# Attention outputs transposed by DMA, a wide warm-up, earlier final waits and one add on POOL in a TensorE-bound attention and feed-forward kernel

## The chip, the cores and the metric

The kernel runs on one core of a Trainium2 chip. The metric is the device time of one execution in microseconds (us). The time of a run is about 1.7 us longer than the span of its trace (580.16 against 578.4 us for the profiled run of the kernel before).

## The reference

For x of 2048 tokens by 576 features, in bfloat16:

```python
xn = _layernorm(x)
s  = A(xn)            # 32 heads of 18, causal window of 256 keys, softmax, then @ wo
g  = silu(B(xn))      # h = sigmoid(xn @ w_gate) * (xn @ w_up); h @ w_down   (F = 4608)
out = x + s * g
```

## The kernel before

The kernel describes its work as a graph of operations, each with an estimated length, and a list scheduler in the kernel itself places them on the engines' in-order queues before anything runs. So a change of one operation can move the order on every engine. Tokens are handled in four chunks of 512, each of four blocks of 128. The core's feed-forward matmuls fill the time in which attention waits. The contraction of 128 rows is split into two halves of 64 rows which TensorE (PE) runs side by side; "a pair" is one matmul on each half.

The parts that the change touches:

```python
# start: warm-up matmuls on zeros, pairs of 256 columns   [NWARM = 60]
zero = self.hT[:, 0, 0:2 * P]
z = op("DVE", 600, lambda e: e.memset(zero, 0.0), "init:zero", prio=0)
for i in range(NWARM):
    ...pair(eng, self.halves(h, 2 * P), lambda r, t: zero[r, 0:P], lambda r, t: zero[r, :], True, True)
    w = op("PE", 220 if i < 18 else 110, f_warm, f"warm:{i}", ...)   # left out once the first real matmul is placed

# end of attention: TensorE transposes each of the four blocks, DVE evicts, then the output projection   [NOT = 2]
tr = op("PE", KB * 29.5, f_tr, f"otr:{qb}", ...)
te = op("DVE", dve_ns(KB * P, 1.9), f_te, f"ote:{qb}", deps=[tr, do], prio=1)
wo = self.row_proj("wo", qb, h2, lambda r, k, so=so: self.oT[r, so, k, :], ..., [te, ...])

# end of a token block: x + s * g, then the store
q3 = op("DVE", dve_ns(w, 2.0), lambda e: e.tensor_tensor(xf, xf, t, ALU.add), f"fq3:{nm}", deps=[q2, o_dx], prio=2)

# end of SyncE's program: wait for every DMA semaphore ("lane")
if e == "SP":
    for i, n in enumerate(lane_cnt):
        if n > 0:
            eng.wait_ge(lanes[i], n)
    eng.nop()
```

The last token block is finished in two column parts of 384 and 192 (`c0 == 0` is the first). One more part matters, though the change does not touch it: the q and k heads are moved into place by 160 small SBUF-to-SBUF DMAs, `qk<-qd`, which **POOL** issues.

```python
o = self.dma(dst, src, ..., f"dma:sp:{c}:{u}:{w}:{gi}", ("qk", par, gi), deps=[ev, war, self.op_qz], prio=1, eng="POOL")
```

The softmax here doesn't subtract the row's maximum and nothing guards it: scores larger than these inputs give would overflow.

Of the kernel before, what the change touches and what calls it, by code (L numbers as in the profile page):

```python
# [5 lines left out]
ALU = mybir.AluOpType  # L6

S = 2048
D = 576
# [21 lines left out]
NVS = 12  # L31
VH = DH + 1
VSZ = (H // 2) * VH
NOT = 2
NQS = 4
NKX = 2
NEX = 8
# [15 lines left out]
NQD = 2  # L53
NFIN = 2
NTAIL = 96
NWARM = 60
PARTS = ((0, 1), (1, 2), (2, 4))
NQK = 5

DMA_ISSUE_NS = {"SP": 640.0, "POOL": 520.0, "ACT": 650.0}  # L60
# [164 lines left out]
class Builder:  # L225
# [153 lines left out]
    def load_x(self, c, i=0):  # L379
        if c == 0:  # L380
            for i in range(BPC):
                self.x_dma[i] = (self.dma(self.x0[:, i, :], self.x[i * P:(i + 1) * P, :], P * D * 2, f"dma:x{i}", ("x0", i), prio=0),
                                 self.x0[:, i, :])
            return
        st = c * BPC + i
        slots, dd = [], []
        for _ in range(2):
            s_, d_ = self.r_xr.produce()
            slots.append(s_)
            dd += d_  # L390
        assert slots[1] == slots[0] + 1
        o = self.dma(self.xr[:, slots[0]:slots[0] + 2, :],
                     self.x[st * P:(st + 2) * P, :].rearrange("(t p) d -> p t d", p=P),
                     2 * P * D * 2, f"dma:x{st}", ("x", slots[0]), deps=[dd, self.hm[6] if c == 1 else None], prio=5)
        o.slack = 5000.0
        for j in range(2):
            self.x_dma[st + j] = (o, self.xr[:, slots[j], :])
# [9 lines left out]
    def build_consts(self):  # L407
        op = self.op
        self.op_negh = op("DVE", 60, lambda e: e.memset(self.neghalf[:, :], -0.5), "init:neghalf", prio=0)
        o1 = op("POOL", 200, lambda e: e.memset(self.ident[:, :], 0.0), "init:ident1", prio=0)  # L410
        o2 = op("POOL", 200, lambda e: e.affine_select(
            self.ident[:, :], self.ident[:, :], pattern=[[1, SW]], compare_op=ALU.not_equal, fill=1.0, base=0,
            channel_multiplier=-1), "init:ident2", deps=[o1], prio=0)
        self.op_ident = op("POOL", 200, lambda e: e.affine_select(
            self.ident[:, :], self.ident[:, :], pattern=[[1, SW]], compare_op=ALU.not_equal, fill=1.0, base=SW,
            channel_multiplier=-1), "init:ident3", deps=[o2], prio=0)
        zero = self.hT[:, 0, 0:2 * P]
        z = op("DVE", 600, lambda e: e.memset(zero, 0.0), "init:zero", prio=0)  # L418
        self.op_tab = op("ACT", 1500, lambda e: e.activation(self.tring[:, 0, 0:1], zero[:, 0:1], ACTF.Exp), "init:tab",
                         deps=[z], prio=0)  # L420
        h = self.pool_f.hold()
        w = None
        for i in range(NWARM):
            def f_warm(eng):
                return pair(eng, self.halves(h, 2 * P), lambda r, t: zero[r, 0:P], lambda r, t: zero[r, :], True, True)
            w = op("PE", 220 if i < 18 else 110, f_warm, f"warm:{i}", deps=[z], prio=4, acq=None if i else h, odeps=[w])
            w.filler = h
            h.release(w)

        wq, wk, wv = (self.wqkv[:, i * D:(i + 1) * D] for i in range(3))  # L430
        self.op_wqk = [self.load_nat(self.wqk[:, :, i, :], w, "dma:wqk", ("wqk", i), 5) for i, w in enumerate((wq, wk))]
        self.op_wqk += self.load_rem(self.wqkr[:, :], (wq, wk), "dma:wqkr", ("wqkr",), 5)
        for o in self.op_wqk:
            o.slack = 2500.0
        self.op_wv = [self.load_nat(self.wv_sb[:, :, :], wv, "dma:wv", ("wv",), 6)]
        self.op_wv += self.load_rem(self.wvr[:, :], (wv[:, 0:288], wv[:, 288:D]), "dma:wvr", ("wvr",), 6)
        for o in self.op_wv:
            o.slack = 5000.0
        self.op_wqk4 = [op("DVE", 420, lambda e: e.tensor_copy(self.wq4[:, 1:KB, :, :], self.wqk[:, :, :, 512:D]), "init:wq4",
                           deps=self.op_wqk, prio=2)]  # L440
        for t in range(2):
            for i in range(2):
                self.op_wqk4.append(op("DVE", 130, lambda e, t=t, i=i: e.tensor_copy(
                    self.wq4[ROWS[t], 0, i, :], self.wqkr[ROWS[i], 512:D]), f"init:wq4:{t}{i}", deps=self.op_wqk, prio=2))
# [24 lines left out]
    def build_ln(self, c):  # L469
# [3 lines left out]
        for i in range(BPC):  # L473
            st = c * BPC + i
            if c and i % 2 == 0:
# [17 lines left out]
            ap = op("DVE", 430, lambda e, ss=ss, x_in=x_in, sn=sn: e.tensor_scalar(  # L493
                self.xnr[:, sn, RD:XW], x_in, self.mv[:, ss, 0:1], self.rstd[:, ss, :],
                ALU.subtract, ALU.mult), f"ln:ap:{st}", deps=[rs, ag, dn], prio=pr)
            if c:
                dup = op("DVE", 180, lambda e, sn=sn: e.tensor_copy(self.xnr[:, sn, 0:RD], self.xnr[:, sn, RD:2 * RD]),
                         f"ln:dup:{st}", deps=[ap], prio=pr)
            else:
                dup = op("POOL", 260, lambda e, ss=ss, x_in=x_in, sn=sn: e.tensor_scalar(  # L500
                    self.xnr[:, sn, 0:RD], x_in[:, 0:RD], self.mv[:, ss, 0:1], self.rstd[:, ss, :],
                    ALU.subtract, ALU.mult), f"ln:dup:{st}", deps=[rs, ag, dn], prio=pr)
            if c:
                self.r_xr.release(i % 2, ap)
            self.r_st.release(ss, ap)
            self.r_st.release(ss, dup)
            if c:
                fl = self.flip(self.xnT[:, xs, :, i * P:(i + 1) * P], self.xnr[:, sn, :], f"flip:x:{st}", ("fx", xs, i),
                               deps=[dup, war], prio=2)
# [278 lines left out]
    def build_wo(self, c):  # L788
# [3 lines left out]
                 deps=[self.op_on[(c, 0)], self.otr_last], prio=1)  # L792
        for i in range(BPC):
            qb = c * BPC + i
            h = self.pool_s.hold()
            so, do = self.r_oT.produce()

            def f_tr(eng, i=i, h=h):
                return self.transposes(eng, h, lambda r, o: self.o_tok[r, i, o:o + P])
            tr = op("PE", KB * 29.5, f_tr, f"otr:{qb}", deps=[[self.op_on[(c, hg)] for hg in range(NHG)], dup, self.op_ident, do],  # L800
                    prio=1, acq=h)
            last.append(tr)

            def f_te(eng, h=h, so=so):
                dst = self.oT[:, so, :, :].rearrange("p k (t c) -> p t k c", t=2)
                return eng.tensor_copy(dst, self.tr_src(h))
            te = op("DVE", dve_ns(KB * P, 1.9), f_te, f"ote:{qb}", deps=[tr, do], prio=1)
            h.release(te)

            h2 = self.pool_s.hold()  # L810
            ss = i
            war = [self.op_q2[qb - BPC]] if c else []

            wo = self.row_proj("wo", qb, h2, lambda r, k, so=so: self.oT[r, so, k, :], self.wo_sb, self.wor,
                               [te, self.op_wo_w, war])
            self.r_oT.release(so, wo)

            def f_se(eng, ss=ss, h2=h2):
                dst = self.s_attn[:, ss, :].rearrange("p (t c) -> p t c", t=2)
                return eng.activation(dst, self.both(h2, 288), ACTF.Copy, scale=0.25)  # L820
            se = op("ACT", act_ns(D), f_se, f"sev:{qb}", deps=[wo], prio=1)
            h2.release(se)
            self.op_s[qb] = se
        self.otr_last = last

    def build_ffn(self, c):
# [40 lines left out]

        def gate_up(ft, h, half, acq, part=None, deps=()):
            sw, fc = slots[ft // WG], slice((ft % WG) * P, (ft % WG + 1) * P)
            b0, b1 = (0, BPC) if part is None else PARTS[part]  # L870
            t0, n = b0 * P, (b1 - b0) * P
            xin = self.op_xnT[c][b0:b1]

# [24 lines left out]
        if early:  # L898
            weights(0)
            weights(1)  # L900
            hs = [self.pool_f.hold() for _ in range(2)] + [self.pool_s.hold()]
            his = [None] * early
            for part in range(len(PARTS)):
                los = [gate_up(ft, hs[ft], 0, None if part else hs[ft], part, [his[ft]]) for ft in range(early)]
                for ft in range(early):
                    u = his[ft] = gate_up(ft, hs[ft], 1, None, part, [los[ft]])
                    if part == len(PARTS) - 1:
                        tail(ft, hs[ft], u)
                    if part == len(PARTS) - 1 and ft == 1:
                        self.r_w.release(slots[0], u)  # L910
        for ft in range(early, NFT):
            if ft % WG == 0 and ft // WG not in slots:
                weights(ft // WG)
# [50 lines left out]
    def build_final(self, sb, h, f2, c0=0, n=288):  # L964
# [36 lines left out]
            h.release(w0)  # L1001
            h.release(th1)
        self.op_q2[sb] = q2
        q3 = op("DVE", dve_ns(w, 2.0), lambda e: e.tensor_tensor(xf, xf, t, ALU.add), f"fq3:{nm}", deps=[q2, o_dx], prio=2)  # L1004
        self.r_th.release(st, q3)
        if c0 == 0:
            self.fq3 = []
# [99 lines left out]
    def emit(self):  # L1107
# [10 lines left out]
        for e in ENGS:  # L1118
            for o in self.prog[e]:
# [5 lines left out]
                else:  # L1125
                    cnt[e] += 1
                    o.tok = (("E", e), cnt[e])

        def semof(key):
            return lanes[key[1]] if key[0] == "L" else self.sem[key[1]]  # L1130

        def run_engine(e, eng):
            known = {}
            for o in self.prog[e]:
                waits = {}
                for d in o.deps:
                    k, v = d.tok
# [8 lines left out]
                if o.needs_tok:  # L1146
                    ins.then_inc(semof(o.tok[0]), 16 if o.lane is not None else 1)
            if e == "SP":
                for i, n in enumerate(lane_cnt):
                    if n > 0:  # L1150
                        eng.wait_ge(lanes[i], n)
                eng.nop()

        with nc.Block() as block:
# [61 lines left out]
```

## Time and profile before

| | before |
|---|---|
| time, median of 4 runs (3 at the time of the prediction: 579.93) | 580.25 us |
| span of the trace | 578.4 us |
| PE busy | 569.9 us |
| first, last matmul start | 1.15, 573.51 us |
| last matmul start to end of program | 4.9 us |

From the page of the kernel before: the span; busy time with share of the span and number of instructions; the granted clock in tenths over 40 slices; and the shares of the chain that ended last.

```profile
span 578.4 us, 21485 instructions
...
PE 569.9 (99%) x9542; PEld 362.2 (63%) x9542; DVE 345.5 (60%) x837; ACT 267.8 (46%) x379; POOL 179.9 (31%) x290
...
PEclk9999999999999999999999999999999999999999
...
PE 97%; DVE 2%; issue 1%; ACT 0%; POOL 0%; DVEq 0%
```

PE is busy nearly throughout and is nearly the whole chain. The ends of matmuls in a profile are modelled, so the busy share alone doesn't show lost time, and I also read PE's start-to-start steps in the trace: 108 ns for a matmul of 64x512 and 61 ns for 64x288, two at a time, with only about 9.5 us lost over the whole run.

The attention-output transposes, from the view of the tile o_tok (durations in ns as minimum, median, maximum; then first and last start in us):

```profile
L550 PE MATMUL ps<-ident,o_tok x160: 186/190/199, 114.0 to 451.7; 64*128 64x64 bf16 x160
```

The profile gives each a length of 190 ns, but they start 14.5 ns apart, so 160 of them take 2.3 us of PE.

The start, from PE's timeline (start us, length us, engine, line, operation, count, and in brackets the idle time before):

```profile
10.74 1.07 PE L98 MATMUL ps<-xnT,wgs 64*128 64x128 bf16 x31
12.73 0.21 PE L98 MATMUL ps<-xnT,wgs 64*128 64x128 bf16 x1 [0.92 <-issue]
12.86 0.29 PE L98 MATMUL ps<-xnT,wgr 64*128 64x256 bf16 x2
```

PE stops from 11.6 us until 12.73 us with no releaser named. Before this, PE runs warm-up matmuls on zeros: in this trace a pair starts every 0.213 us at first and every 0.109 us from 5.0 us on. I call that halving of the step the release of the clock.

The tail, from the timeline of all engines:

```profile
573.08 0.56 DVE L999 SCALAR_TENSOR_TENSOR thf<-thf,s_attn 128x384 bf16<-128x384 bf16 x1
573.67 0.36 DVE L1004 TENSOR_TENSOR xf<-xf,thf 128x384 bf16<-128x384 bf16 x1
...
573.95 0.60 DVE L994 TENSOR_TENSOR s_attn<-s_attn,ps 128x96 bf16<-128x96 bf16 x2
...
574.98 0.26 DVE L1004 TENSOR_TENSOR xf<-xf,thf 128x192 bf16<-128x192 bf16 x1
575.26 0.34 SPq L254 DMA_DIRECT2D out_dram<-xf  x1
```

The 384-column add (0.36 us on DVE, at 573.67) stands before the last block's work in DVE's queue. The last output is issued at 575.26 us and the program ends at 578.42, 3.16 us later.

Two waits of SyncE (SP) at the end (total us, times, longest us), the second being the wait of the closing barrier for the other engines:

```profile
SPq L1151 <- DMA out_dram<-xf: 0.6, 1, 0.6
SPq L1154 <- PEq L1154: 0.2, 1, 0.2
```

Last, a view that I did not ask for before predicting, and should have: the closing line of the program, on which every engine's sequencer executes a DRAIN, the instruction with which the engine's program closes here (ns, then start us); and POOL's last working instruction, from its timeline.

```profile
L1154 POOLq DRAIN  x1: 8982/8982/8982, 389.6 to 389.6; - x1
...
L1154 DVEq DRAIN  x1: 297/297/297, 575.0 to 575.0; - x1
...
L1154 SPq DRAIN  x1: 13/13/13, 578.2 to 578.2; - x1
...
389.64 0.40 POOL L670 COPY kprev<-qk 128x256 bf16<-128x256 bf16 x1 [6.62 <-DVE kx L666]
```

DVE and SP drain in 0.3 us or less. POOL's DRAIN is 8982 ns long. The copy runs inside it and ends at 390.04 us; the DRAIN ends at 398.60, 8.56 us later. It costs nothing here because POOL has no work after 390 us and the program ends at 578 us.

### The profile page before, as it was taken

Reading aid. Unit: us, or ns where it says so; the run is one execution under the profiler, and the core shown is the slowest. Engines: PE = TensorE matmul, PEld = TensorE weight load, DVE = VectorE, ACT = ScalarE, POOL = GpSimd, SP = SyncE. Lnnn points to the kernel's source line nnn. Section 1 sums busy time; section 2 is a strip of 40 time slices with the busy share of each in tenths; the row PEclk is TensorE's granted clock in tenths of the full one; section 3 lists DMA queues with packets and bytes.
Section 4 is the critical chain, followed back from the end, with each engine's and each line's share of the span. In section 5 each row is a group of like instructions: output and inputs, shape, how many; then the busy total and the mean of one; then the engine's idle time right before and its main releaser. Section 6 shows DMA issues by size and latency. Waiting matters only on the chain.

```text
span 578.4 us, 21485 instructions
## 1 busy us (share of the span) xinstructions
PE 569.9 (99%) x9542; PEld 362.2 (63%) x9542; DVE 345.5 (60%) x837; ACT 267.8 (46%) x379; POOL 179.9 (31%) x290
## 2 busy tenths in 40 slices
PE   8999999999999999999999999999999999999996
PEld 7555455678985556555788875555457754444786
DVE  4478989845899775577876578877321133333123
ACT  2247568421676653856663566685221023232111
POOL 7466454107564443145534354340000000000000
PEclk9999999999999999999999999999999999999999
DMA  8978865922313433333611023343340015442010
GB/s 241 272 200 202 223 188 159 213 46 55 90 51 95 133 94 110 93 92 96 116 36 43 19 57 105 108 119 111 114 144 22 23 58 152 132 141 74 2 43 23
DMA packets 104908, 62.06 MB, mean 107 GB/s; under 512 B 15308, under 2 KB 103452, under 8 KB 104816
## 3 DMA queue, kind: packets, MB, share of 16 engines
q1 hardware_dynamic: 99696, 55.95, 35.4%
q0 software_dynamic: 5120, 4.74, 3.3%
q8 instruction: 75, 1.23, 0.9%
q14 instruction: 17, 0.14, 0.1%
HBM read 51.61 MB, written 2.36 MB: 93 GB/s over the span
## 4 chain that ended last, share of the span: by engine, by line
PE 97%; DVE 2%; issue 1%; ACT 0%; POOL 0%; DVEq 0%
PE ps L98 96%; DVE hT L890 1%; PE ps L550 1%; ACT tring L887 0%; DVE pvs L767 0%; DVE s_attn L994 0%; DVE thf L999 0%; DVE xf L1004 0%; POOL small L488 0%; DVE expr L714 0%; DVE xnr L493 0%; DVE small L465 0%; DVE pvs L771 0%; DVE hT L418 0%; DVE small L486 0%
## 5 line engine op out<-in xcount | busy, mean ns | idle before, releaser
L98 PE MATMUL ps<-xnT,wgs 64*128 64x512 bf16 (+2 forms) x2400 | 288.4, 368 | 1.0 <-issue 0.9
L98 PEld LDWEIGHTS ps<-xnT,wgs 64*128 64x128 bf16 x2400 | 111.7, 94 | 113.7 <-PE ps L98 1.6
L701 ACT ACTIVATE expr<-ps 128x1024 bf16<-128x1024 f32 (+2 forms) x160 | 156.2, 983 | 52.1 <-PE ps L98 51.6
L98 PE MATMUL ps<-wd_sb,hT 64*128 64x288 bf16 (+2 forms) x2448 | 154.9, 276 | 0.0
L887 ACT ACTIVATE tring<-ps 128x512 bf16<-128x512 f32 x144 | 85.7, 596 | 130.4 <-PE ps L98 128.0
L890 DVE SCALAR_TENSOR_TENSOR hT<-tring,ps 128x512 bf16<-128x512 bf16 x144 | 98.5, 685 | 79.4 <-ACT tring L887 77.3
L98 PEld LDWEIGHTS ps<-wd_sb,hT 64*128 64x128 bf16 x2448 | 118.0, 94 | 22.3
L254 POOL DMA_DIRECT2D qk<-qd x160 | 82.2, 523 | 86.6 <-DVE qd L588 48.7
L666 POOL TENSOR_SCALAR kx<-kprev,small 128x256 bf16<-128x256 bf16 x64 | 64.8, 1023 | 72.1 <-PE ps L98 71.7
L714 DVE TENSOR_TENSOR expr<-expr,mask 128x256 bf16<-128x256 bf16 (+2 forms) x232 | 64.9, 301 | 29.8 <-ACT expr L701 28.4
L767 DVE TENSOR_REDUCE pvs<-ps 64x304 f32<-64x608 f32 x64 | 50.4, 787 | 17.5 <-PE ps L98 16.3
L98 PE MATMUL ps<-qk,kx 64*128 64x320 bf16 (+4 forms) x736 | 59.9, 251 | 0.0
L98 PE MATMUL ps<-xnT,wgr 64*128 64x512 bf16 (+2 forms) x300 | 55.9, 368 | 1.4 <-DVE hT L890 1.2
L98 PEld LDWEIGHTS ps<-qk,kx 64*128 64x128 bf16 x736 | 31.7, 94 | 25.2 <-ACT expr L701 1.7
L984 ACT ACTIVATE thf<-ps 128x576 bf16<-128x576 f32 (+3 forms) x22 | 11.4, 519 | 70.1 <-PE ps L98 69.5
L98 PEld LDWEIGHTS ps<-v_aug,expr 64*128 64x128 bf16 x2432 | 35.5, 93 | 6.2 <-issue 0.2
L98 PE MATMUL ps<-v_aug,expr 64*128 64x19 bf16 (+1 forms) x2432 | 35.9, 170 | 0.0
L98 PE MATMUL ps<-xnT,wqk 64*128 64x512 bf16 x256 | 32.0, 376 | 0.0
L588 DVE CAST qd<-ps 128x1024 bf16<-128x1024 f32 (+1 forms) x20 | 22.1, 1116 | 7.7 <-PE ps L98 7.5
L666 DVE TENSOR_SCALAR kx<-qk,small 128x512 bf16<-128x512 bf16 x64 | 23.5, 388 | 5.3 <-DMA qk<-qd 4.6
L987 DVE SCALAR_TENSOR_TENSOR thf<-thf,ps 128x576 bf16<-128x576 bf16 x12 | 9.1, 754 | 29.3 <-ACT thf L984 28.7
L98 PEld LDWEIGHTS ps<-xnT,wgr 64*128 64x128 bf16 x300 | 14.9, 94 | 15.4 <-DVE hT L890 3.4
(66 smaller groups left out, 293.8 us busy)
## 6 DMA issues: line engine op xcount, KB each, us to landing
wgs<-in_B_w_gate_dram SPq DMA_DIRECT2D x72, 256.0 KB, 3.1
wgs<-in_B_w_up_dram SPq DMA_DIRECT2D x72, 256.0 KB, 3.5
wd_sb<-in_B_w_down_dram SPq DMA_DIRECT2D x9, 576.0 KB, 4.9
qk<-qd POOLq DMA_DIRECT2D x100, 36.0 KB, 2.0
xf<-in_A_x_dram SPq DMA_DIRECT2D x16, 144.0 KB, 2.8
out_dram<-xf SPq DMA_DIRECT2D x16, 144.0 KB, 1.8
xr<-in_A_x_dram SPq DMA_DIRECT2D x6, 288.0 KB, 3.8
wqk<-in_A_wqkv_dram SPq DMA_DIRECT2D x2, 576.0 KB, 6.6
```

The costliest lines, as they stand in the source:

```text
L98: res = eng.matmul(outs[i], lhs(ROWS[t], i), rhs(ROWS[t], i), start=start, stop=stop, tile_position=(64 * t, 0))
L254: o = self.op(eng, DMA_ISSUE_NS[eng], lambda e: e.dma_start(dst, src), name, deps, prio, nbytes=nbytes)
L550: res = eng.transpose(self.psb[:, o:o + 64], src(r, k * P), self.ident[r, :], tile_position=(64 * t, 0))
L588: return eng.tensor_copy(dst, self.both(h, n))
L666: return e.tensor_scalar(self.kx[:, sx, pos:pos + n_ // SW, t, :], src.rearrange("p (s k) -> p s k", k=SW), self.half[:, t:t + 1], None, A ...
L701: return eng.activation(self.expr[:, se, :, lo * SW:NT], self.both(h, NT)[:, :, lo * SW:NT], ACTF.Exp, scale=SM_SCALE)
L714: return eng.tensor_tensor(e_, e_, m_, ALU.mult)
L767: return eng.tensor_reduce(out[ROWS[i]], src, mybir.AxisListType.X, ALU.add)
L887: th = op("ACT", act_ns(NT), lambda e: e.activation(self.tring[:, st, :], bank(h, 0), ACTF.Tanh, scale=0.5), f"th:{c}:{ft}", deps=[pg, dt_ ...
L890: mu = op("DVE", dve_ns(NT), lambda e: e.scalar_tensor_tensor(self.hT[:, ft, :], self.tring[:, st, :], 1.0, bank(h, 1), ALU.add, ALU.mult) ...
L984: return e.activation(v2(t)[:, a:b, :], y2()[:, a:b, :], ACTF.Tanh, scale=0.25)
L987: q1 = op("DVE", dve_ns(w), lambda e: e.scalar_tensor_tensor(v2(t), v2(t), 1.0, y2(), ALU.add, ALU.mult), f"fq1:{nm}", deps=[th, f2], prio=0)
```

## The change

The intent: take the output transposes off the busy PE and give them to the DMA queues; warm the clock with fewer, wider matmuls and finish the early feed-forward tiles one after another; move the waits for old DMAs ahead of the last output; and relieve DVE of one add at the end by giving it to POOL. `XPRIO = 0` multiplies a priority that was 0, so it changes nothing.

```diff
-NOT = 2
+NOT = 4
-NWARM = 60
-PARTS = ((0, 1), (1, 2), (2, 4))
+NWARM = 36
+PARTS = (((0, 1), (1, 2), (2, 4)), ((0, 1), (1, 2), (2, 4)), ((0, 2), (2, 4)))
...
-        zero = self.hT[:, 0, 0:2 * P]
+        zero = self.hT[:, 0, :]
...
-                return pair(eng, self.halves(h, 2 * P), lambda r, t: zero[r, 0:P], lambda r, t: zero[r, :], True, True)
-            w = op("PE", 220 if i < 18 else 110, f_warm, ...)
+                return pair(eng, self.halves(h, NT), lambda r, t: zero[r, 0:P], lambda r, t: zero[r, :], True, True)
+            w = op("PE", 432 if i < 9 else 216, f_warm, ...)
...   # layer norm of chunk 0: the copy of 64 columns on DVE, as in the other chunks, not on POOL
-            if c:
-                dup = op("DVE", 180, ...)
-            else:
-                dup = op("POOL", 260, ...)
+            dup = op("DVE", 180, ...)
...
-            h = self.pool_s.hold()
             so, do = self.r_oT.produce()
-            ...
-            tr = op("PE", KB * 29.5, f_tr, f"otr:{qb}", ...)
-            ...
-            te = op("DVE", dve_ns(KB * P, 1.9), f_te, f"ote:{qb}", deps=[tr, do], prio=1)
-            h.release(te)
+            te = self.flip(self.oT[:, so, :, :], self.o_tok[:, i, :], f"flip:o:{qb}", ("fo", so),
+                           deps=[[self.op_on[(c, hg)] for hg in range(NHG)], dup, do])
...   # the three early gate/up tiles one after another, not part by part
-            for part in range(len(PARTS)):
-                los = [gate_up(ft, hs[ft], 0, ...) for ft in range(early)]
-                ...
+            for ft, h in enumerate(hs):
+                u = None
+                for part in range(len(PARTS[ft])):
+                    lo = gate_up(ft, h, 0, None if part else h, part, [u])
+                    u = gate_up(ft, h, 1, None, part, [lo])
+                tail(ft, h, u)
...
-        q3 = op("DVE", dve_ns(w, 2.0), lambda e: e.tensor_tensor(xf, xf, t, ALU.add), f"fq3:{nm}", deps=[q2, o_dx], prio=2)
+        big = w < D and c0 == 0
+        q3 = op("POOL" if big else "DVE", 700 if big else dve_ns(w, 2.0), lambda e: e.tensor_tensor(xf, xf, t, ALU.add), f"fq3:{nm}",
+                deps=[q2, o_dx], prio=2)
...   # SyncE: wait for all lanes but the outputs' before the last instruction, for the outputs' after it
+                if e == "SP" and o is self.prog[e][-1]:
+                    for i, n in enumerate(lane_cnt):
+                        if n > 0 and i not in outs:
+                            eng.wait_ge(lanes[i], n)
...
-                for i, n in enumerate(lane_cnt):
-                    if n > 0:
-                        eng.wait_ge(lanes[i], n)
+                for i in outs:
+                    eng.wait_ge(lanes[i], lane_cnt[i])
```

More of the change, by code (lines that the diff above doesn't have):

```diff
@@ L55 @@
 NTAIL = 96
-NWARM = 60
-PARTS = ((0, 1), (1, 2), (2, 4))
+NWARM = 36
+PARTS = (((0, 1), (1, 2), (2, 4)), ((0, 1), (1, 2), (2, 4)), ((0, 2), (2, 4)))
+XPRIO = 0
 NQK = 5
@@ L381, in load_x @@
             for i in range(BPC):
-                self.x_dma[i] = (self.dma(self.x0[:, i, :], self.x[i * P:(i + 1) * P, :], P * D * 2, f"dma:x{i}", ("x0", i), prio=0),
+                self.x_dma[i] = (self.dma(self.x0[:, i, :], self.x[i * P:(i + 1) * P, :], P * D * 2, f"dma:x{i}", ("x0", i), prio=XPRIO * (i > 1)),
                                  self.x0[:, i, :])
@@ L424, in f_warm @@
             def f_warm(eng):
-                return pair(eng, self.halves(h, 2 * P), lambda r, t: zero[r, 0:P], lambda r, t: zero[r, :], True, True)
-            w = op("PE", 220 if i < 18 else 110, f_warm, f"warm:{i}", deps=[z], prio=4, acq=None if i else h, odeps=[w])
+                return pair(eng, self.halves(h, NT), lambda r, t: zero[r, 0:P], lambda r, t: zero[r, :], True, True)
+            w = op("PE", 432 if i < 9 else 216, f_warm, f"warm:{i}", deps=[z], prio=4, acq=None if i else h, odeps=[w])
             w.filler = h
@@ L495, in build_ln @@
                 ALU.subtract, ALU.mult), f"ln:ap:{st}", deps=[rs, ag, dn], prio=pr)
-            if c:
-                dup = op("DVE", 180, lambda e, sn=sn: e.tensor_copy(self.xnr[:, sn, 0:RD], self.xnr[:, sn, RD:2 * RD]),
-                         f"ln:dup:{st}", deps=[ap], prio=pr)
-            else:
-                dup = op("POOL", 260, lambda e, ss=ss, x_in=x_in, sn=sn: e.tensor_scalar(
-                    self.xnr[:, sn, 0:RD], x_in[:, 0:RD], self.mv[:, ss, 0:1], self.rstd[:, ss, :],
-                    ALU.subtract, ALU.mult), f"ln:dup:{st}", deps=[rs, ag, dn], prio=pr)
+            dup = op("DVE", 180, lambda e, sn=sn: e.tensor_copy(self.xnr[:, sn, 0:RD], self.xnr[:, sn, RD:2 * RD]),
+                     f"ln:dup:{st}", deps=[ap], prio=pr)
             if c:
@@ L505, in build_ln @@
             self.r_st.release(ss, ap)
-            self.r_st.release(ss, dup)
             if c:
@@ L794, in build_wo @@
             qb = c * BPC + i
-            h = self.pool_s.hold()
             so, do = self.r_oT.produce()
-            def f_tr(eng, i=i, h=h):
-                return self.transposes(eng, h, lambda r, o: self.o_tok[r, i, o:o + P])
-            tr = op("PE", KB * 29.5, f_tr, f"otr:{qb}", deps=[[self.op_on[(c, hg)] for hg in range(NHG)], dup, self.op_ident, do],
-                    prio=1, acq=h)
-            last.append(tr)
-            def f_te(eng, h=h, so=so):
-                dst = self.oT[:, so, :, :].rearrange("p k (t c) -> p t k c", t=2)
-                return eng.tensor_copy(dst, self.tr_src(h))
-            te = op("DVE", dve_ns(KB * P, 1.9), f_te, f"ote:{qb}", deps=[tr, do], prio=1)
-            h.release(te)
+            te = self.flip(self.oT[:, so, :, :], self.o_tok[:, i, :], f"flip:o:{qb}", ("fo", so),
+                           deps=[[self.op_on[(c, hg)] for hg in range(NHG)], dup, do])
+            last.append(te)
             h2 = self.pool_s.hold()
@@ L869, in gate_up @@
             sw, fc = slots[ft // WG], slice((ft % WG) * P, (ft % WG + 1) * P)
-            b0, b1 = (0, BPC) if part is None else PARTS[part]
+            b0, b1 = (0, BPC) if part is None else PARTS[ft][part]
             t0, n = b0 * P, (b1 - b0) * P
@@ L901, in build_ffn @@
             hs = [self.pool_f.hold() for _ in range(2)] + [self.pool_s.hold()]
-            his = [None] * early
-            for part in range(len(PARTS)):
-                los = [gate_up(ft, hs[ft], 0, None if part else hs[ft], part, [his[ft]]) for ft in range(early)]
-                for ft in range(early):
-                    u = his[ft] = gate_up(ft, hs[ft], 1, None, part, [los[ft]])
-                    if part == len(PARTS) - 1:
-                        tail(ft, hs[ft], u)
-                    if part == len(PARTS) - 1 and ft == 1:
-                        self.r_w.release(slots[0], u)
+            for ft, h in enumerate(hs):
[4 more added lines that the diff above has]
+                tail(ft, h, u)
+                if ft == 1:
+                    self.r_w.release(slots[0], u)
         for ft in range(early, NFT):
@@ L1127, in emit @@
                     o.tok = (("E", e), cnt[e])
+        outs = [i for lane, i in self.lane_ids.items() if lane[0] == "out"]
         def semof(key):
```

## The prediction

> **What bounds it now.** The page shows PE busy 569.9 of 578.4 us at full granted clock; the chain of work that ended last is 97% PE. By start-to-start times in the trace, 64x512 matmuls come every 108 ns, 64x288 every 61 ns: two row halves run together and the array is full. Only about 9.5 us are lost between first (1.15 us) and last matmul (573.5 us): 3.8 in the first 40 us, the rest in small waits (largest 0.8 us, near 104 us). The tail after it is 4.9 us.
>
> **What changes.**
>
> 1. *Transposes.* 160 TensorE transposes leave, 14.5 ns each start-to-start: 2.3 us off a full PE. 16 copies to oT leave DVE (60% busy, no gain). Sixteen DMA transposes come. The 12 already there take 1.26 us of queue and land in a median 4.0 us (largest 6.1). Of four in a row the last should land about 9 us after attention ends. In the new order 18 PE steps or more stand between the last probability-value product and the first output projection, so I expect them hidden. The Trainium skill ("DMA: Bandwidth & Descriptors", Latency and other measured facts) gives DMA transposes 261 GB/s; 160 KB would be an estimated 0.65 us, so landing is mostly latency. Transposes also stop claiming PSUM.
>
> 2. *Start.* Cold warm-up pairs now start every 0.213 us until 4.96 us, 3.8 us after the first. The skill ("TensorE: Matmul & The Clock Gate", Part 1) says that the budget is time, not a number of matmuls; so I expect 0.427 us per wide pair until about 5 us. Fifteen pairs then end near 6.4 us; the first x transpose starts there instead of at 5.88, the first real matmul near 8.9 instead of 8.49: 0.4 us lost. But 20 fewer pairs are 80 fewer PE instructions. The timeline shows PE stopped from 11.6 to 12.73 us with "issue" named; all that it needed was there by 11.4, and a 16 KB instruction fetch was in flight from 10.33 to 11.47. I read this as a fetch stall; with fewer and wider matmuls before it, it should shrink to 0.3 us or less. Finishing the early tiles one after another also frees PSUM earlier (waits of 0.28 and 0.22 us near 17 us). Net: -0.8 us.
>
> 3. *Tail.* The last output lands near 577.05; the remaining queue waits, 0.06 us per pair, run until 577.96. They move ahead of the last output: -0.9 us. The 384-column add on POOL frees DVE of 0.36 us and starts the last block 0.18 us earlier; on POOL, estimated at 0.7 to 1.2 us from its 128x256 copies (0.4) and scalings (1.0), it is just hidden. Together -1.0 us.
>
> 4. *Middle.* A new order reshuffles 5 us of small waits: -0.4, give or take 1.5.
>
> **Sum.** -2.3 -0.8 -1.0 -0.4 = -4.5: **575.4 us**, range 573.5 to 578.0. Chances: faster by over 2% 0.01, within 2% 0.98, slower 0.01.
>
> **What would show it.** No o_tok transposes on PE and its matmul steps 2.3 us shorter in sum; no stop near 11 to 13 us; last matmul to end 3.9 us, not 4.9; 28 DMA transposes, output projections not waiting for them.
>
> **What would make it wrong.** The sync queue is in order: a DMA transpose waiting for attention holds back weight loads behind it, and PE starves (gate/up matmuls waiting on DMA). Transposes could land later behind weight traffic. The fetch stall could move rather than vanish. POOL's add could finish last.

## The result, and the profile after

The changed kernel takes 582.74 us (median of 4 runs, 581.62 to 582.89) against 580.25 us for the kernel before (4 runs, 579.84 to 580.60). The ratio of the fast runs is 1.0039 with a 95% interval of 1.0022 to 1.0056: a little slower, within 2%, and outside the predicted range of 573.5 to 578.0 us. A ratio, here and below, is the mean time of one kernel's fast runs over that of the other's of the same batch, so it is not quite the ratio of the medians quoted.

| | before | after |
|---|---|---|
| span of the trace | 578.4 us | 579.9 us |
| last matmul start | 573.51 us | 569.96 us |
| last output issued | 575.26 us | 571.66 us |
| end of program | 578.42 us | 579.88 us |
| last matmul start to end of program | 4.9 us | 9.9 us |

PE finished 3.55 us earlier, and the last output was issued 3.6 us earlier. All of the loss, and more, is in the stretch behind them.

The page after, the same lines as before:

```profile
span 579.9 us, 21062 instructions
...
PE 567.0 (98%) x9324; PEld 357.8 (62%) x9324; DVE 339.3 (59%) x824; ACT 268.2 (46%) x379; POOL 177.3 (31%) x287
...
PEclk9999999999999999999999999999999999999998
...
PE 93%; DVE 2%; DMA 1%; issue 1%; ACT 1%; POOL 1%; DVEq 0%
```

The only slice with a granted clock under 0.9 is the span's last, in which PE is idle. The mean clock of this run, 0.995, is lower than before for that slice; it is not a cause.

The output transposes, from the view of the tile oT (the last line is the time from issue to landing, in us):

```profile
L260 SPq DMA_TRANSPOSE oT<-o_tok x16: 1202/1282/1534, 111.0 to 402.3; - x16
...
DMA to landing us min/median/max: 2.6/3.7/8.1
```

They land after a median 3.7 us; in that view PE's matmuls that read oT show no wait for a DMA.

The start: no stop of a microsecond is left. By the steps of the matmuls, the largest pauses between 10 and 16 us are of 0.2 to 0.4 us, one of them before 12.39 us.

```profile
11.41 0.84 PE L99 MATMUL ps<-xnT,wgs 64*128 64x128 bf16 x16
12.39 0.28 PE L99 MATMUL ps<-xnT,wgr 64*128 64x256 bf16 x2
12.51 0.60 PE L99 MATMUL ps<-xnT,wgs 64*128 64x256 bf16 x8
```

The tail:

```profile
569.52 0.56 DVE L983 SCALAR_TENSOR_TENSOR thf<-thf,s_attn 128x384 bf16<-128x384 bf16 x1
570.16 0.91 POOL L989 TENSOR_TENSOR xf<-xf,thf 128x384 bf16<-128x384 bf16 x1 [188.71 <-DVE thf L983]
...
570.20 0.61 DVE L978 TENSOR_TENSOR s_attn<-s_attn,ps 128x96 bf16<-128x96 bf16 x2
...
571.32 0.26 DVE L989 TENSOR_TENSOR xf<-xf,thf 128x192 bf16<-128x192 bf16 x1
571.66 0.34 SPq L255 DMA_DIRECT2D out_dram<-xf  x1
```

The add takes 0.91 us on POOL and is done at 571.07, before DVE's last add at 571.32 to 571.58. DVE starts the last block's work 0.68 us after the 384-column `thf` starts, where it took 0.87 us before: the gain of 0.18 us that was forecast is there too. So far all is as predicted.

SP's last waits:

```profile
SPq L1145 <- PEq L1145: 6.2, 1, 6.2
...
SPq L1143 <- DMA out_dram<-xf: 1.4, 1, 1.4
```

The closing barrier of SP now waits 6.2 us, where it waited 0.2. The view puts it down to PE's sequencer, but PE's own DRAIN was over by 570.2 us, so it must be another engine. The view of the closing line tells which:

```profile
L1145 POOLq EVENT_SEMAPHORE  x2: 17/17/17, 579.7 to 579.8; - x2
...
L1145 POOLq DRAIN  x1: 9531/9531/9531, 570.1 to 570.1; - x1
...
L1145 DVEq DRAIN  x1: 297/297/297, 571.3 to 571.3; - x1
...
L1145 SPq DRAIN  x1: 13/13/13, 573.7 to 573.7; - x1
```

The last output lands near 573.4 us and SP drains at 573.7. POOL's DRAIN started at 570.12 us and took 9531 ns, to 579.65. Its first 0.95 us hold the add; the other 8.58 us come after the add's end, against 8.56 us after the last copy in the kernel before. The same DRAIN has moved from 390 us, where it was hidden, to the end of the program.

### The profile page after: what moved, and what is told of

It reads as the page before. It is cut to its first block, busy times and chain, and to the rows that moved or that the text cites. A ratio compares the mean times of both kernels' runs of the same rounds, so it can differ in the third digit from the quotient of the medians.

```text
span 579.9 us, 21062 instructions
## 1 busy us (share of the span) xinstructions
PE 567.0 (98%) x9324; PEld 357.8 (62%) x9324; DVE 339.3 (59%) x824; ACT 268.2 (46%) x379; POOL 177.3 (31%) x287
## 4 chain that ended last, share of the span: by engine, by line
PE 93%; DVE 2%; DMA 1%; issue 1%; ACT 1%; POOL 1%; DVEq 0%
PE ps L99 93%; DMA qk<-qd 1%; DVE hT L875 1%; POOL qk L255 1%; ACT tring L872 1%; DVE qd L583 0%; DVE pvs L762 0%; ACT xnT L522 0%; ACT expr L696 0%; DVE kx L661 0%; PE ps L545 0%; DVE s_attn L978 0%; DVE thf L983 0%; DVE hT L419 0%; DVE xf L989 0%
```

## The experiments

Two theories stood at first. Theory D: the closing DRAIN of POOL is what the chip waits for, and the add on POOL is what brought it there. Rival T: the sixteen new DMA transposes, or their completion, hold up the end.

### The add back on DVE (e1_add_on_dve, and again as e1b_add_on_dve)

```diff
 # against the changed kernel
-        q3 = op("POOL" if big else "DVE", 700 if big else dve_ns(w, 2.0), ...)
+        q3 = op("DVE", dve_ns(w, 2.0), ...)
```

> The changed kernel with one thing undone: the 384-column add of the last token block goes back from POOL to DVE; the order on every other engine is unchanged. Theory D (drain): in the changed kernel the chip waits for POOL's closing DRAIN, which ends 8.58 us after POOL's last instruction (571.07 to 579.65 us) while everything else is done at 573.7; with no late POOL work the DRAIN goes back to about 381 us, hidden, and the span becomes about 574.2 us, the time about 575.9 us (575.2 to 576.6), some 4.3 us below the kernel before. Rival T (transposes): the sixteen extra DMA transposes, or their completion, hold up the end of the program; then undoing the add leaves the time within 1 us of 582.7 us.

Measured: 576.08 us (6 runs), ratio 0.9929 (0.9907 to 0.9951). POOL's and SP's DRAIN, from the view of the closing line:

```profile
L1143 POOLq DRAIN  x1: 8981/8981/8981, 381.8 to 381.8; - x1
...
L1143 SPq DRAIN  x1: 13/13/13, 574.6 to 574.6; - x1
```

The DRAIN is back at 381.8 us, and the program ends 2.25 us after the last output is issued (572.55 to 574.80). Theory D's figure was 575.9.

> The same kernel as in the first experiment, beside the one with fewer warm-up pairs on the same chip: 576.0 us (575.5 to 576.6), 0.72% under the kernel before, the POOL drain hidden.

Measured on another chip: 576.62 us (6 runs), ratio 0.9927 (0.9907 to 0.9947), within 0.02% of the first ratio, though the median lies just above the expected 575.5 to 576.6 us.

### Only the add on POOL (e2_before_pool_add)

```diff
 # against the kernel before
-        q3 = op("DVE", dve_ns(w, 2.0), ...)
+        big = w < D and c0 == 0
+        q3 = op("POOL" if big else "DVE", 700 if big else dve_ns(w, 2.0), ...)
```

> The kernel before with that one part of the change added: the 384-column add of the last block on POOL, nothing else. Theory D: POOL's last instruction ends near 574.6 us, its DRAIN 8.6 us later, so the span is about 583.4 us against 578.4 and the time about 585 us, 5 us slower (4.3 to 5.6). Rival T: no DMA transposes of outputs here, so the time stays within 0.5 us of 580.2 us.

Measured: 585.56 us (4 runs), ratio 1.0082 (1.0061 to 1.0104). The add on POOL, and the same lines:

```profile
573.93 0.91 POOL L1005 TENSOR_TENSOR xf<-xf,thf 128x384 bf16<-128x384 bf16 x1 [183.68 <-DVE thf L999]
...
L1156 POOLq DRAIN  x1: 9529/9529/9529, 573.9 to 573.9; - x1
...
L1156 SPq DRAIN  x1: 13/13/13, 578.4 to 578.4; - x1
```

The add ends at 574.84 us and the DRAIN 8.58 us later. There is no output transpose by DMA in this kernel. Rival T falls, and the add alone costs 5.3 us here by the medians.

### Any late instruction on POOL? (d1_tiny_late_pool)

```diff
 # against e1 (add on DVE)
+        if w < D and c0 == 0:
+            op("POOL", 120, lambda e: e.memset(self.ident[:, 0:1], 0.0), "late", deps=[q2], prio=2)
```

> The add is on DVE, but POOL gets one late instruction that does nothing useful: a memset of one column (0.1 us) that waits for the same value as the add did. If any late POOL instruction exposes the drain: memset near 570.3 us, DRAIN ends 8.6 us after it, span about 579.2 us, time about 581 us, nearly all of the loss back. If it is the add itself (its size, its operation, its shared operands) that makes the drain long: DRAIN under 1 us and span about 574.3 us.

Measured (one run, 582.34 us, span 580.6 us). POOL's timeline at the end:

```profile
571.70 0.10 POOL L990 MEMSET ident<- 128x1 bf16 x1 [188.69 <-DVE thf L983]
```

and the closing line again:

```profile
L1145 POOLq DRAIN  x1: 8681/8681/8681, 571.7 to 571.7; - x1
...
L1145 SPq DRAIN  x1: 13/13/13, 575.4 to 575.4; - x1
```

A memset of one column that nobody needs brings the loss back: 8.56 us from its end (571.80) to the end of the DRAIN (580.36). For these two, an add of 384 columns and a memset of one, the size and kind of the late instruction make no difference to what follows it.

### What sets the length of the DRAIN (d2, d3, d4, d5, d6)

All five are the changed kernel with the late add on POOL, where some of the 160 moves `qk<-qd` are issued by ACT in place of POOL. Each is a single run of one trace. Their times (583.30, 581.73, 586.96, 585.19 and 589.91 us for d2, d3, d4, d5 and d6) are not used, since ACT's queue delays everything else.

```diff
-                             deps=[ev, war, self.op_qz], prio=1, eng="POOL")
+                             deps=[ev, war, self.op_qz], prio=1, eng="ACT")                              # d2: 0 moves on POOL
+                             ..., eng="POOL" if gi == 4 else "ACT")                                      # d3: 32
+                             ..., eng="POOL" if gi < 3 else "ACT")                                       # d4: 96
+                             ..., eng="POOL" if gi < 4 else "ACT")                                       # d5: 128
+                             ..., eng="POOL" if gi < 2 else "ACT")                                       # d6: 64
```

> The changed kernel, with the late add on POOL, but all 160 moves qk<-qd are issued by ACT and none by POOL. If the closing DRAIN is the price of POOL having issued software DMAs: DRAIN ends under 1 us after the add, as the one at the start of the program (0.17 us, no DMA before it). If it is a fixed price of closing POOL: 8.6 us after the add again. The time itself says little, ACT is loaded otherwise.

With no move issued by POOL (the add, and POOL's DRAIN on the closing line, whose length includes the 0.95 us in which the add starts and runs; the add takes 0.91 us in the four runs after this one too):

```profile
577.81 0.91 POOL L989 TENSOR_TENSOR xf<-xf,thf 128x384 bf16<-128x384 bf16 x1 [140.04 <-DVE thf L983]
...
L1145 POOLq DRAIN  x1: 1017/1017/1017, 577.8 to 577.8; - x1
```

> As the run with the moves on ACT, but the 32 moves of the last projection group stay on POOL, 128 go to ACT. If the DRAIN grows with the number of moves that POOL issued: 8.6 x 32/160 = 1.7 us after the add. If it is there in full once any was issued (or regardless): 8.6 us. If it has a fixed and a proportional part: between.

With 32:

```profile
L1145 POOLq DRAIN  x1: 3651/3651/3651, 576.1 to 576.1; - x1
```

> As the runs with the moves on ACT, but POOL keeps the 96 moves of the first three projection groups (3.15 MB of the 4.72 MB) and ACT takes 64. Measured so far, from the end of POOL's last instruction to the end of its DRAIN: 0.07 us with no move issued by POOL, 2.70 us with 32 moves (0.52 MB), 8.56 to 8.58 us with 160 (4.72 MB). If the DRAIN grows with the number of moves (46 ns each between these two): 5.6 us. If it grows with their bytes (1.4 us per MB between these two): 6.4 us. If it is set by something else, another value.

With 96:

```profile
L1145 POOLq DRAIN  x1: 8877/8877/8877, 576.0 to 576.0; - x1
```

Neither of the two values expected here came: not by number from two points (5.6), nor by bytes (6.4). The four values known by then looked like a line through 0, 32 and 96 moves, with 160 off it. Two more runs tested that.

> POOL keeps the 64 moves of the first two projection groups, ACT takes 96. Line of 82 ns a move through the runs with 0, 32 and 96 moves: the DRAIN ends 5.3 us after the add. If the length follows something else, such as the number of semaphores that the moves signal (4 here, 2, 6 and 10 before): about 5.3 as well only by chance.

With 64:

```profile
L1145 POOLq DRAIN  x1: 6264/6264/6264, 581.6 to 581.6; - x1
```

> POOL keeps the 128 moves of the first four projection groups, ACT takes 32. If the line is capped, near the 8.57 us of 160 moves: 8.57 us. If the line goes on and the case of 160 is special: 10.5 us. If it is a curve that flattens slowly: between 7.93 and 8.57 us, near 8.3.

With 128:

```profile
L1145 POOLq DRAIN  x1: 11489/11489/11489, 571.7 to 571.7; - x1
```

| moves that POOL issued | 0 | 32 | 64 | 96 | 128 | 160 |
|---|---|---|---|---|---|---|
| end of POOL's last instruction to end of DRAIN, us | 0.07 | 2.70 | 5.31 | 7.93 | 10.54 | 8.58 |

From 0 to 128 moves this is a straight line of 82 ns a move ((10.54 - 0.07) / 128), to within 0.03 us. The DRAIN's length goes with the DMAs that POOL has issued; it is paid when the program closes, and not for time that they need then: in the changed kernel the last of them was issued at 377.5 us and the last packet of POOL's DMA queue started at 378.8, almost 200 us before. It is not a matter of bytes: the 32 moves of d3 carry 0.53 MB and cost 2.63 us, while in d6, d4 and d5 each group of 32 carries 1.05 MB and costs 2.62 us. But three counts rise together in these runs, so they don't tell which one sets the length: the moves, their packets (32 a move in every trace) and the semaphores that they signal (2 for every 32 moves). The expectation for 64 moves calls an agreement of the semaphore count chance; it is not, since 4 semaphores at the same slope also give 5.3 us. No run gave the moves another number of semaphores or packets. The case of 160 is off the line, at what 104 moves would cost. A cap is not the answer, since 128 moves cost more than 160. What happens between 128 and 160 stays open.

### The early final waits alone (e3_before_early_waits)

```diff
 # against the kernel before: only the two blocks of the change in SyncE's program
```

> The kernel before with only the early final waits. If the sum of the prediction is right in this term: the last output lands near 577.05 us as before and the program ends about 0.9 us earlier, span near 577.5 us, time near 579.3 us (0.7 to 1.0 us less). If the waits were already hidden behind something else that ends last, no change within 0.2 us.

Measured: 579.70 us (6 runs), ratio 0.9986 (0.9969 to 1.0004). By the medians this is 0.5 us less, short of the expected 0.7 to 1.0, but the time alone does not resolve it. The trace does (the last output, and SP's DRAIN):

```profile
575.38 0.34 SPq L254 DMA_DIRECT2D out_dram<-xf  x1
...
L1159 SPq DRAIN  x1: 13/13/13, 577.4 to 577.4; - x1
```

The last output is issued at 575.38 us and the program ends at 577.62, 2.24 us later, where it took 3.16 us before. The term is 0.92 us, as predicted. Other traces repeat it: 3.16 or 3.17 us with the old waits (e4, e5, e6), and 2.25 us with the early ones where no DRAIN of POOL is exposed (e1, e1b, e7, d2).

### The DMA transposes alone (e4_before_dma_transposes)

```diff
 # against the kernel before
-NOT = 2
+NOT = 4
 # and flip(...) in place of the TensorE transposes and their evictions, as in the change
```

> The kernel before with only the sixteen output transposes moved to DMA and four buffers. If the transposes are pure load on a full PE and the DMA ones are hidden: 2.3 us less, and the reshuffle of small waits adds plus or minus 1 us: time 577.5 us (576.5 to 578.7). If Rival T holds, or if the in-order queue starves PE of weights: as slow as the kernel before or slower.

Measured: 578.31 us (6 runs), ratio 0.9966 (0.9943 to 0.9990), 1.9 us less by the medians. This agrees with 2.3 us plus a reshuffle. The weights did not starve: the lists of waits of PE and of its weight loads in this trace name no DMA.

### The start alone (e5_before_start), a shorter warm-up (e7_short_warm), a narrower one (e6_narrow_warm)

```diff
 # e5, against the kernel before: NWARM, PARTS, the wide zero tile, the copy on DVE, the early tiles in turn
 # e7, against e1: three warm-up pairs ahead of the first x transpose left out, all else in the same order
+        gone = [o for o in self.prog["PE"] if o.name in ("warm:12", "warm:13", "warm:14")]
+        self.prog["PE"] = [o for o in self.prog["PE"] if o not in gone]
 ...   # and they are taken out of the dependencies of the others
 # e6, against the kernel before: twice as many pairs of half the width
-        zero = self.hT[:, 0, 0:2 * P]
+        zero = self.hT[:, 0, 0:P]
-NWARM = 60
+NWARM = 120
```

To compare starts I use the lag: the time at which a matmul starts, less the sum of undisturbed steps of all useful matmuls before it (no warm-up, no transposes). Its value at 40 us tells what the start cost.

> The kernel before with only the change of the start: wide warm-up, the three early tiles one after another, the copy of 64 columns on DVE. In the whole change the start gained 0.88 us by 40 us (lag of the useful matmuls). If that is the start's own: time 579.3 us (578.6 to 580.1), no stop of PE over 0.5 us between 11 and 15 us. Fetch theory: the stop that stood at the 449th recorded PE instruction in four kernels with the old start stays near that instruction number, now behind wider matmuls, and is 0.2 to 0.5 us. If instead the gain needs the new order that comes with the DMA transposes: no gain.

Measured: 579.68 us (6 runs), ratio 0.9975 (0.9953 to 0.9997), 0.7 us less by the medians. Its trace, however, does not show a gain against the trace of the kernel before: the lag at 40 us is 10.46 us against 10.34. The stop is gone, but the clock was released late. In the steps of the warm-up pairs (0.427 us cold, 0.216 warm):

| trace | clock released, us | first x transpose, us | lag at 40 us |
|---|---|---|---|
| before (narrow) | 5.0 | 5.91 | 10.34 |
| changed (wide, 15 pairs) | 4.2 | 5.94 | 9.46 |
| e1 (the same start) | 6.0 | 6.85 | 10.06 |
| e1b (the same start) | 6.2 | 6.99 | 10.20 |
| e5 (the same start) | 6.8 | 7.26 | 10.46 |
| e7 (wide, 12 pairs) | 4.3 | 5.65 | 9.22 |

The release is given to about 0.2 us, as pairs step; the trace's own record of the granted clock agrees within 0.1 us. By that record it comes between 2.9 and 5.9 us after the first pair in all sixteen traces. It varies with the narrow start too: 3.8 us after the first pair in the kernel before, the earliest of its kind, and 5.0 to 5.8 in e2, e3, e4 and e6. So the comparison of e5 with the kernel before is one of a late release with an early one. Where the narrow start had a late release as well, its lag at 40 us was 10.7 us (e2, released at 6.2) and 10.6 (e3, at 6.9), against 10.06 and 10.46 for the wide start at about the same times (e1, e5); in e4, whose stop was short, it was 9.9. So the start's gain is between 0.9 us and nothing from run to run.

> The changed kernel with the add back on DVE and three of the fifteen wide warm-up pairs ahead of the first x transpose left out; all else in the same order. Two traces of the same start show the tensor clock released 2.9 us (4.2) and 4.7 us (5.95) after the first pair; in the late case the fifteen pairs end 0.7 us later and everything after is 0.6 us later. If the fixed number of wide pairs is what makes late releases costly: 0.5 us less on average and a smaller spread, time 575.5 us (575.0 to 576.2). If the start then waits for the weights anyhow: same as with fifteen pairs, 576.0.

Measured: 575.94 us (6 runs), ratio 0.9920 (0.9899 to 0.9941), beside 576.62 us and 0.9927 for e1b on the same chip. By the medians this is 0.7 us better, but the intervals overlap and the spread (575.49 to 577.47) is no smaller, so the shorter warm-up is not shown to help. Its trace also fell on an early release. It is the fastest version measured, and both it and e1 beat both kernels.

> The kernel before with warm-up pairs of 128 columns, twice as many, so more PE instructions ahead of the same work. Fetch theory: the stop stays near the 449th recorded PE instruction, so it comes earlier in the work (before the third x transpose or in the first gate and up matmuls), and it is 1 us or longer, as those instructions pass faster. Rival: PE stopped at 11.6 us for the data of the third and fourth token block (evictions end at 11.3 us); then the stop stays at the same place in the work, before the first 256-column matmul, whatever the instruction number.

PE's timeline (one run):

```profile
9.23 0.40 PE L98 MATMUL ps<-xnT,wgs 64*128 64x128 bf16 x8
10.34 0.23 PE L98 MATMUL ps<-xnT,wgr 64*128 64x128 bf16 x2 [0.71 <-issue]
```

PE last started a matmul at 9.41 us and the next at 10.34, a stop of 0.93 us, just under the 1 us expected. The stop came 2.2 us earlier than in the kernel before, at another place in the work, and again right after the 449th recorded PE instruction, where it stands in the kernel before (1.14 us), e2 (1.50 us), e3 (1.05 us) and, small, e4 (0.34 us). The rival, a wait for data, would have left it at its place in the work. An instruction fetch of 16 KB was in flight from 7.91 to 8.80 us here, as from 10.33 to 11.47 before. In all five traces it had landed before PE stopped, by 0.1 us (e2) to 1.1 us (e4), so the stop doesn't coincide with the transfer; but PE resumed 1.3 to 1.6 us after the landing each time, and the early fetch of e4 (landed at 10.77 us) goes with its short stop. In the changed kernel the fetch landed at 11.62 us, and PE came to its 449th instruction at 14.48. In the kernels with the new start the nearest pause, 0.33 us, stands after the 460th instruction, and in e7, with 12 fewer instructions, after the 448th: it moves with the work and so is taken for another wait.

## Why the prediction was wrong

| term of the sum | predicted, us | measured, us | by |
|---|---|---|---|
| transposes off PE | -2.3 | -2.3 of PE steps; e4 alone -1.9 | steps in the trace; e4 |
| start | -0.8 | -0.88 in the trace of the change; about 0 to -0.9 from run to run | lag at 40 us; e1, e1b, e2, e3, e5 |
| reshuffled waits | -0.4 | -0.3 | lag from 40 us to the end, less 2.3 |
| early final waits | -0.9 | -0.9 | e3 |
| the add on POOL | -0.1, "just hidden" | +5.3 alone; in the change +5.8 by the tails of the traces, +6.7 by the medians | e2; e1 against the change |

**The failed step is point 3, the tail**: "The 384-column add on POOL frees DVE of 0.36 us and starts the last block 0.18 us earlier; on POOL, estimated at 0.7 to 1.2 us ..., it is just hidden. Together -1.0 us." The add itself was sized rightly (0.91 us) and was hidden. What the step left out is that the last instruction of POOL fixes when POOL's closing DRAIN can end, and that this DRAIN takes another 8.6 us in a program in which POOL has issued its 160 DMAs (0.07 us in d2, where it had issued none). The stretch from the last matmul's start to the end of the program became 9.9 us, not the predicted 3.9. With the add back on DVE it is 4.1 us (570.73 to 574.80), and the time, 576.08 us, lies 0.7 us from the predicted 575.4. In the last row, +5.8 us is the difference of these two tails, 9.9 - 4.1; +6.7 us is the difference of the medians, 582.74 - 576.08, of different rounds, and so is less sure. Alone (e2) the add costs less, 5.0 us by the tails (9.9 against 4.9), because there the old final waits end at 578 us and hide part of the DRAIN.

**The list of what could go wrong named the culprit for the wrong reason.** "POOL's add could finish last" was there, but the add did not finish last; the DRAIN behind it did. The number was in the trace of the kernel before: 8982 ns on POOL's closing line. I took it for granted that an engine's end is the end of its last instruction.

**The transposes were right.** 28 DMA transposes are there, o_tok is no longer transposed on PE, and no wait of PE for their DMA is listed. The fear that the in-order queue starves PE of weights did not come true: PE's last matmul started 3.55 us earlier. For the DMA transposes themselves, the Trainium skill's 261 GB/s ("DMA: Bandwidth & Descriptors", Latency and other measured facts) gave the prediction an estimate of 0.65 us for a block of 160 KB (it is nearer 0.63), and the trace has a median of 3.7 us from issue to landing. No run isolates the rate itself. By this estimate most of the landing time is not transfer, as predicted, but it is not one fixed latency either: seven of the sixteen land in 2.6 or 2.7 us, the first four in 5.8 to 8.1 us, and how much of that is waiting behind other traffic is not separated. The measured duration is the one to plan with.

**The start was right in size, but by luck of one trace.** The prediction took the release of the clock at about 5 us as fixed. The Trainium skill ("TensorE: Matmul & The Clock Gate", Part 1) says that the warm-up is a matter of time and that the transition lies around 4 us, 0.5 us either way; the sixteen traces here show 2.9 to 5.9 us after the first pair, a wider spread. Fifteen wide pairs in an in-order queue take up to 6.4 us if the release is late (15 x 0.427), and the first transpose stands behind them.

**The fetch stall was probably right.** It stands at a fixed instruction number and not at a place in the work (e6), and it is not seen with the new start. That a fetch of instructions is what PE waits for remains an inference from its position and from the resumption 1.3 to 1.6 us after a fetch has landed; what fills that time is not shown, and no run changed the fetch alone. The Trainium skill ("Runtime: NRT & Kernel Launch", Instruction fetch mechanics) calls the crossing of a 16 KB boundary "mostly hidden"; if this is that, it was not hidden here, with small matmuls at 14 ns an instruction just before.

## What to carry to other kernels

An engine is not finished with its last instruction: look at the length of each engine's closing DRAIN in the trace before giving it late work. If POOL has issued DMAs, leave it idle at the end: here one column set to zero by POOL at the end brought the same 8.6 us as a real add. Letting another queue issue them takes the DRAIN away (0.07 us in d2), but is not shown to gain time: with ACT issuing all of them, the one run took 583.30 us. And when a rarely used engine gets a job at the end because it "has time", ask what its end triggers, not only how long the job takes.

## What the Trainium skill lacked or had wrong

- "VectorE: DVE Perf Modes", The DRAIN you can't avoid, tells two kinds of DRAIN apart, the flush after a DVE operation and one from the runtime's preamble and postamble, which it gives as about 12 ns, constant, on all five engines. The closing DRAIN here, which the profile books on the kernel's own line, is described by neither: SP's is 13 ns, but DVE's and ACT's are 0.3 us, PE's 0.66 us, and POOL's ends 0.07 to 10.54 us after POOL's last instruction.
- No page that I found says that POOL's closing DRAIN grows with the DMAs that POOL has issued: 82 ns for each of these moves (each 32 packets) from 0 to 128, and 8.58 us at 160, below the 10.54 us at 128, which no run explains.
- "TensorE: Matmul & The Clock Gate", Part 1, gives the release of the clock with a spread of 0.5 us either way around 4 us, though it also warns that the number of cold matmuls varies from run to run; sixteen traces here show 2.9 to 5.9 us after the first matmul pair.
- "Runtime: NRT & Kernel Launch", Instruction fetch mechanics: crossing a boundary "mostly hidden"; a stop that is best explained by a fetch took 0.93 to 1.50 us in four of the five traces that show it at the 449th instruction, and 0.34 us in the fifth. What it lacks is the time from the landing of a fetch to the next instruction: PE resumed 1.3 to 1.6 us after it.
- "DMA: Bandwidth & Descriptors" gives a bandwidth for DMA transposes (261 GB/s) but no time from issue to landing; for single blocks of 160 KB the changed kernel's trace has 3.7 us in the median, 2.6 to 8.1 us.
